# Two transformer layers with windowed attention on one core: projections of the second chunk on two PSUM banks, even score units in the first chunk, and a planner with four other durations and another table of priorities

## The chip, the core and the metric

The kernel runs on one core of a Trainium2 chip. The core has a matrix engine (TensorE, PE in the profile; its weight loads are listed apart as PEld), a vector engine (VectorE, DVE), a scalar engine (ScalarE, ACT), a general engine (GpSimd, POOL) and a queue engine (SyncE, SP) that issues nearly all DMAs here. Matmul results land in PSUM, eight banks of 512 fp32 columns on 128 partitions. The metric is the device time of one execution in microseconds (us). Three runs of the kernel before took 881.19, 881.58 and 882.57 us; the median is 881.58.

## The reference

The input x has 2048 rows of 576 numbers in bf16. Two layers with the same weights follow each other, each made of a mixer and an MLP:

```python
def _A_ref(x, wqkv, wo):                     # H = 32 heads of Dh = 18, window W = 256
    qkv = (x @ wqkv).reshape(B, S, 3, H, Dh).transpose(2, 0, 3, 1, 4)
    q, k, v = qkv[0], qkv[1], qkv[2]
    scores = einsum("bhqd,bhkd->bhqk", q, k) * Dh ** -0.5
    scores = where((i - j >= 0) & (i - j < W), scores, -1e9)
    o = einsum("bhqk,bhkd->bhqd", softmax(scores), v)
    return o.transpose(0, 2, 1, 3).reshape(B, S, D) @ wo
def _B_ref(x, w1, b1, w2, b2):               # F = 4608
    return gelu(layernorm(x) @ w1 + b1) @ w2 + b2
x = x + _A_ref(layernorm(x)); x = x + _B_ref(layernorm(x))     # twice
```

`_B_ref` normalizes once more inside, so that the MLP's input is normalized twice; the kernel does both in one step.

## The kernel before

**Tiles and chunks.** The rows are 16 tiles of 128. Four tiles make a chunk, and the two layers together make eight chunks, numbered k = 0 to 7; chunks 0 and 4 are the first of their layers. The residual stream stays on the chip in fp32 (`x_res`), and the weights of the MLP are streamed in from memory again for each chunk (`w1_load`, `w2_load`).

**Stages of a chunk.** `ln1` or `ln1_in` normalizes the four tiles (statistics on DVE at L678 and L682, the reciprocal root on POOL at L691 and L693, the normalized copy on DVE at L703, a second copy of its last 64 columns at L711, and a transposing DMA by SP at L727). `qkv` makes the projections of a tile: for each of q, k and v two outputs of 288 columns, each in a bank of its own. Chunks 0 and 1 use `two_out` (five matmuls of 128 rows for each output, L763); later chunks use two row halves of the array at once (L803). DVE takes each output out of its bank (L824 for q and k, L811 for v), and SP transposes q and k by DMA (L843). `E0` (chunk 0) and `E` (all others) do the attention for eight groups g of four heads: `scores` is one unit of work, up to 512 query columns for each of four heads (PE at L870), two exponentials on ACT (L879), each over two heads, and the masking of the blocks on the diagonal and at the window's far edge on POOL (L900). `pv` multiplies the weights by v (PE at L917), and DVE transposes and divides (L928, L931, L934, L938). `tail` multiplies by `wo` (L763), adds the residual (L980) and normalizes again for the MLP. `G_part` is a third of the first MLP matmul (L1033) with its gelu on ACT (L1043), `mm2` a third of the second (L1071) with its residual add on DVE (L980, at the very end L983).

**Banks.** Each unit of scores takes two pairs of banks out of three, (0,1), (2,3) and (4,5). The outputs of `pv` take one of 7, 6, 5, 4 in that order of preference, and so do projections, `tail` and `mm2`. For chunk 1 alone the projections may take nothing but bank 6, so that each output waits until DVE has emptied the one ahead of it. `G_part` may take any of the eight.

**The planner.** Nothing in the order is written out by hand. Each operation is added as a task with an engine, what it reads and writes, an assumed duration (`cost`, us), a latency and a priority. `Plan.schedule` then plays the kernel through with these durations: at each step it takes the task that can start first, and among those that start at the same time the one with the lowest priority number. PE tasks are of four kinds, `f` (whole array), `h` (two row halves), `r` (four row strips, the scores) and `c` (four column strips, `pv`); a change of kind is assumed to cost 0.095 us, and from 40 us on a table `PL.turn` adds a handicap to tasks that would change it. `PL.nudge` adds a number to the priority of each stage. Its keys are stage names: `ea2.1` is group 1 in the first part of the attention of chunk 2 (`ea`, `eb` and `ec` hold groups 0 to 2, 3 to 5, 6 and 7), `ea2.p1` its `pv`; `q2.1` the projections of tile 1 of chunk 2; `t2.1` the tail of that tile; `ga`, `gb`, `gc` and `ma`, `mb`, `mc` the three parts of the two MLP matmuls; `ln2` a normalization; a `+` marks the weight loads. What comes out is a fixed order for each engine; on the chip each engine runs through its own order and waits on semaphores. Where PE would be idle for long in the first 140 us, the planner puts in matmuls on zeros (L665).

**Units of the first chunk.** `units_of` cuts the scores of one group. In a middle chunk there are three units of 512 columns. In the first chunk of a layer the parts that would look back at rows before the start are dropped, and units of 384, 512 and 256 columns are left.

Of the kernel before, what the change touches and what calls it, by code (L numbers as in the profile page):

```python
# [417 lines left out]
def build_kernel(nc, A_x, A_wqkv, A_wo, B_x, B_w1, B_b1, B_w2, B_b2, out):  # L418
# [37 lines left out]
    PL = Plan(S, 8)  # L456
# [4 lines left out]
    PL.nudge = {"": -255.24, "b": -219.8, "ea0.0": 23.65, "ea0.1": -0.79, "ea0.2": 6.45, "ea0.p0": -38.42, "ea0.p1": 20.22,  # L461
# [88 lines left out]
    oq = sb("oq", [P, 16, 32], FP32)  # L550
# [3 lines left out]
    xn = sb("xn", [P, NXN, KD * 128], BF16)  # L554
# [710 lines left out]
```

## Time and profile before

One execution was profiled. It took 880.89 us, 0.69 us less than the median of the three runs; the profile's span is 879.2 us, and 1.69 us lie around it.

| Quantity | Value |
|---|---|
| Profiled execution | 880.89 us, span 879.2 us |
| PE busy | 861.2 us (98%), 9675 matmuls |
| ACT busy | 596.3 us (68%) |
| DVE busy | 414.2 us (47%) |
| POOL busy | 367.8 us (42%) |
| PE busy in the first 100 us | 91.03 us |
| PE busy from 100 to 865 us | 758.83 of 765 us |
| Granted TensorE clock | 1.00 throughout |

A busy share is the time in which an instruction of that engine was under way; matmuls overlap, so a PE that is always busy may still lose time at changes of kind. "Idle before" gives how long the engine stood still ahead of an instruction and which other engine's instruction ended that. An instruction's duration in the profile is longer than the step from one to the next where two of the same engine overlap.

### The profile page before, as it was taken

How to read it: one execution, taken by the hardware profiler on the slowest of the kernel's cores; microseconds unless marked ns; L12 is line 12 of the kernel's file. 1: busy time of each engine (PE TensorE's matmuls, PEld its weight loads, DVE VectorE, ACT ScalarE, POOL GpSimd, SP SyncE). 2: the span in 40 equal slices, each digit the busy share in tenths (PEclk: the TensorE clock that was granted, in tenths of full speed). 3: DMA queues.
4: the chain of work that ended last, by engine and by line, in shares of the span. 5: the costliest groups of instructions: out<-in, count | busy, mean ns of one | idle time of the engine just before them, and what ended most of it. 6: DMA issues, size and time to landing. Idle time of an engine off the chain costs nothing.

```text
span 879.2 us, 23104 instructions
## 1 busy us (share of the span) xinstructions
PE 861.2 (98%) x9675; PEld 507.4 (58%) x9675; DVE 414.2 (47%) x994; ACT 596.3 (68%) x741; POOL 367.8 (42%) x500
## 2 busy tenths in 40 slices
PE   9898999999999999999999999999999999999998
PEld 7444555556566565566655555655556555556665
DVE  6889423664237632476433943374233533262111
ACT  5976788858757696565774868729768589753443
POOL 3766554465234562254420845416444176231100
PEclk9999999999999999999999999999999999999999
DMA  7698435361585524936356262584425953445341
GB/s 193 141 196 187 113 114 135 110 165 52 163 164 126 136 63 157 181 108 179 103 131 186 62 180 84 150 174 111 155 82 136 226 123 104 136 130 171 104 159 50
DMA packets 181847, 119.53 MB, mean 136 GB/s; under 512 B 107440, under 2 KB 181744, under 8 KB 181744
## 3 DMA queue, kind: packets, MB, share of 16 engines
q1 hardware_dynamic: 181744, 118.05, 52.0%
q8 instruction: 77, 1.26, 0.6%
q14 instruction: 26, 0.21, 0.1%
HBM read 90.10 MB, written 2.36 MB: 105 GB/s over the span
## 4 chain that ended last, share of the span: by engine, by line
PE 80%; DVE 7%; DMA 4%; ACT 4%; issue 3%; POOL 2%; SPq 0%; DVEq 0%; POOLq 0%
PE ps L1033 31%; PE ps L1071 28%; PE ps L803 9%; PE ps L870 5%; PE ps L917 4%; PE ps L763 4%; ACT pT L879 3%; DVE xn L703 2%; DMA xnTm<-xn 2%; POOL pT L900 1%; DVE st_all L678 1%; DVE xn L711 1%; DMA xnTa<-xn 1%; DVE x_res L980 1%; ACT hT L1043 1%
## 5 line engine op out<-in xcount | busy, mean ns | idle before, releaser
L900 POOL TENSOR_SCALAR_AFFINE_SELECT pT<-pT 128x512 bf16<-128x512 bf16 (+1 forms) x368 | 287.8, 805 | 271.6 <-ACT pT L879 267.9
L879 ACT ACTIVATE pT<-ps 128x1024 bf16<-128x1024 f32 (+2 forms) x384 | 347.1, 972 | 51.5 <-PE ps L870 51.1
L1071 PE MATMUL ps<-w_sb,hT 128*128 128x288 bf16 x2208 | 298.5, 287 | 3.8 <-DVE x_res L980 2.0
L1043 ACT ACTIVATE hT<-ps,b1col 128x512 bf16<-128x512 f32 x276 | 168.4, 688 | 195.3 <-PE ps L1033 194.6
L1033 PE MATMUL ps<-xnTm,w_sb 64*128 64x512 bf16 x2592 | 292.8, 376 | 0.2 <-ACT pT L879 0.2
L1071 PEld LDWEIGHTS ps<-w_sb,hT 128*128 128x128 bf16 x2208 | 203.2, 98 | 84.6 <-issue 23.7
L1033 PEld LDWEIGHTS ps<-xnTm,w_sb 64*128 64x128 bf16 x2592 | 126.9, 94 | 141.9 <-issue 6.7
L980 DVE TENSOR_TENSOR x_res<-ps,x_res 128x288 f32<-128x288 f32 x224 | 99.1, 446 | 170.1 <-PE ps L1071 136.3
L928 DVE STREAM_TRANSPOSE oq<-ps 128x512 f32<-128x512 f32 x64 | 45.6, 712 | 112.1 <-PE ps L917 111.5
L803 PE MATMUL ps<-wqkv,xnTa 64*128 64x288 bf16 x1296 | 95.4, 283 | 2.5 <-DMA xnTa<-xn 0.9
L824 DVE CAST qn<-ps 128x288 bf16<-128x288 f32 x120 | 49.7, 449 | 80.6 <-PE ps L803 72.5
L803 PEld LDWEIGHTS ps<-wqkv,xnTa 64*128 64x128 bf16 x1296 | 61.1, 94 | 35.0 <-issue 6.4
L870 PE MATMUL ps<-qT,kT 32*128 32x384 bf16 (+2 forms) x1216 | 64.1, 276 | 2.0 <-ACT pT L879 1.7
L691 POOL TENSOR_SCALAR vtmp<-mv_all 128x1 f32<-128x1 f32 (+1 forms) x43 | 8.8, 206 | 130.6 <-DVE mv_all L682 129.1
L1049 POOL TENSOR_TENSOR x_res<-x_res,b2bc 128x576 f32<-128x576 f32 x32 | 40.7, 1293 | 43.8 <-ACT hT L1043 43.8
L678 DVE BATCH_NORM_STATS2 st_all<-x_res 128x6 f32<-128x288 f32 (+1 forms) x128 | 53.7, 443 | 1.7 <-DMA x_res<-in_A_x_dram 1.2
L917 PE MATMUL ps<-pT,vA 128*20 128x384 bf16 (+2 forms) x1408 | 50.4, 276 | 1.0 <-DVE qn L824 0.8
L703 DVE TENSOR_SCALAR xn<-x_res,mv_all,rstd 128x576 bf16<-128x576 f32 (+1 forms) x64 | 43.8, 685 | 13.8 <-DMA xnTm<-xn 5.7
L811 DVE CAST vA<-ps 128x288 bf16<-128x288 f32 x64 | 26.5, 448 | 40.5 <-PE ps L803 38.5
L763 PE MATMUL ps<-wo_sb,attT 128*128 128x288 bf16 x320 | 44.2, 287 | 0.6 <-DVE x_res L980 0.6
L870 PEld LDWEIGHTS ps<-qT,kT 32*128 32x128 bf16 x1216 | 19.4, 92 | 43.1 <-issue 30.3
L917 PEld LDWEIGHTS ps<-pT,vA 128*20 128x20 bf16 x1408 | 25.8, 90 | 23.1 <-issue 11.6
(47 smaller groups left out, 389.7 us busy)
## 6 DMA issues: line engine op xcount, KB each, us to landing
w_sb<-in_B_w_dram SPq DMA_DIRECT2D x48, 864.0 KB, 5.9
w_sb<-in_B_w_dram SPq DMA_DIRECT2D x48, 768.0 KB, 4.7
w_sb<-in_B_w_dram SPq DMA_DIRECT2D x96, 48.0 KB, 4.4
out_dram<-xn SPq DMA_DIRECT2D x16, 144.0 KB, 1.8
wqkv<-in_A_wqkv_dram SPq DMA_DIRECT2D x3, 576.0 KB, 5.3
x_res<-in_A_x_dram SPq DMA_DIRECT2D x3, 576.0 KB, 4.3
wo_sb<-in_A_wo_dram SPq DMA_DIRECT2D x4, 144.0 KB, 3.3
xnTm<-xn SPq DMA_TRANSPOSE x32, 2.6
```

The lines of the kernel that those rows point to most:

```text
L678: add("dve", lambda e, i=i, s=s: e.bn_stats(st_all[:, t, i, :], s[:, t, i * HB:(i + 1) * HB]), reads=res, writes=[f"st{t}_{i}"], cost=0.37 ...
L703: add("dve", lambda e: e.tensor_scalar(xn[:, sl, 0:D], s[:, t, :], mv_all[:, t, 0:1], rstd[:, t:t + 1], op0=ALU.subtract, op1=ALU.mult), r ...
L763: ins = e.matmul(bank(bs[o])[:, 0:HB], lhs(c), rhs(c, o * HB), start=(c == 0), stop=(c == KD - 1))
L803: ins = e.matmul(bank(bs[o])[:, 0:HB], xnTa[r:r + 64, c, i * 128:(i + 1) * 128], wqkv[r:r + 64, c, col:col + HB], start=(c == 4), stop=(ph ...
L870: ins = e.matmul(two(bs[j // 2])[:, j % 2, col:col + nq * 128], k_of(T0 + so)[0][32 * j:32 * j + 32, g, :], qs[32 * j:32 * j + 32, g, qo * ...
L879: add("act", lambda e, h2=h2: e.activation(pT[:, sl, 2 * h2:2 * h2 + 2, lo:hi], two(bs[h2])[:, :, lo:hi], ACT.Exp, scale=SCALE), reads=[bs ...
L900: add("pool", lambda e, ap=ap, pat=pat, sgn=sgn, kind=kind: e.affine_select(ap, ap, pattern=pat, compare_op=(ALU.is_ge if kind == "d" else ...
L917: ins = e.matmul(bank(bo)[32 * j:32 * j + VW, qo * 128:(qo + nq) * 128], vA[:, (T0 + so) % VS, 8 * j + g, :], pT[:, sl, j, col:col + nq * ...
L980: add("dve", lambda e: e.tensor_tensor(x_res[:, t, sl], bank(b)[:, 0:HB], x_old[:, t, sl], ALU.add), reads=[b] + ([f"xin{t}"] if first els ...
L1033: ins = e.matmul(bank(bks[i])[:, 0:n], w1_sb[r:r + 64, sls[i], col:col + 128], xnTm[r:r + 64, k % 2, c, 0:n], start=(c == 4), stop=(ph == ...
L1043: add("act", lambda e, ff=ff, hd=hd, bk=bk: e.activation(hd[:, 0:n], bank(bk)[:, 0:n], ACT.Gelu_apprx_tanh, bias=b1col[:, ff:ff + 1]), rea ...
L1071: ins = e.matmul(bank(b)[:, 0:HB], h_of(k, hf, fl)[0][:, i * 128:(i + 1) * 128], w2_sb[:, fl, hh * HB:(hh + 1) * HB], start=(fl == 0), sto ...
```

## The change

Four things change in the text of the kernel.

1. The projections of chunk 1 may take bank 6 or bank 7, not bank 6 alone.
2. In the first chunk of each layer (t0 = 0, chunks 0 and 4) the units of a group are 384, 384 and 384 columns: the 128 columns of the part (3, 3) move from the second unit to the third.
3. Assumed durations in the planner: the normalized copy at L703 from 0.67 to 0.53 us (from fp32) and from 0.45 to 0.43 us (from the bf16 input), its second copy at L711 from 0.38 to 0.24 us, the division of the attention's output at L934 from 0.60 to 0.45 us, the gelu at L1043 from 0.145 to 0.125 us plus 0.00087 us a column (at 512 columns from 0.590 to 0.570 us). The instructions themselves are the same.
4. The whole table `PL.nudge` is another one: 465 entries in place of 476, of which 48 have the value they had, nearly all of them for the last two chunks.

```diff
-    PL.nudge = {"": -255.24, "b": -219.8, "ea0.0": 23.65, "ea0.1": -0.79, "ea0.2": 6.45, "ea0.p0": -38.42, "ea0.p1": 20.22,
...
+    PL.nudge = {"": -3.97, "b": 31.08, "ea0.0": 10.46, "ea0.1": 43.28, "ea0.2": -4.02, "ea0.p0": 39.43, "ea0.p1": -87.35,
...
-            reads=res + [f"mv{t}", f"rstd{t}"], writes=[f"xn{sl}"], cost=0.67 if src is None else 0.45, lat=0.14, prio=prio)
+            reads=res + [f"mv{t}", f"rstd{t}"], writes=[f"xn{sl}"], cost=0.53 if src is None else 0.43, lat=0.14, prio=prio)
...
-                reads=res + [f"mv{t}", f"rstd{t}"], writes=[f"xd{sl}"], cost=0.38, lat=0.14, prio=prio)
+                reads=res + [f"mv{t}", f"rstd{t}"], writes=[f"xd{sl}"], cost=0.24, lat=0.14, prio=prio)
...
-                             wr, prio + 0.01 * n, after=dest, fill=(6,) if k == 1 else FILL)
+                             wr, prio + 0.01 * n, after=dest, fill=(6, 7) if k == 1 else FILL)
...
             us = [[(0, 0, 2, 0), (1, 1, 1, 256)], [(-1, 0, 2, 0), (-2, 0, 1, 256)]]
+        if t0 == 0:
+            us = [[(0, 0, 3, 0)], [(1, 1, 3, 128)], [(2, 2, 2, 256), (3, 3, 1, 128)]]
         us = [[p for p in u if t0 + p[0] >= 0] for u in us]
...
-            reads=["oq", f"ri{r}"], writes=[f"aq{g}"], cost=0.6, lat=0.14, prio=prio - 3)
+            reads=["oq", f"ri{r}"], writes=[f"aq{g}"], cost=0.45, lat=0.14, prio=prio - 3)
...
-                    reads=[bk, "b1"], writes=..., cost=0.145 + n * 0.00087, lat=0.17,
+                    reads=[bk, "b1"], writes=..., cost=0.125 + n * 0.00087, lat=0.17,
```

More of the change, by code (lines that the diff above doesn't have):

```diff
@@ L1044, in G_part @@
                                                                       bias=b1col[:, ff:ff + 1]),
-                    reads=[bk, "b1"], writes=[hn] + ([f"p{fl // 4}{x}" for x in ("h0", "h1", "m0", "m1", "m2")] if hn[1] == "p" else []), cost=0.145 + n * 0.00087, lat=0.17,
+                    reads=[bk, "b1"], writes=[hn] + ([f"p{fl // 4}{x}" for x in ("h0", "h1", "m0", "m1", "m2")] if hn[1] == "p" else []), cost=0.125 + n * 0.00087, lat=0.17,
                     fifo="act", prio=prio)
```

140 rows, old and new, of the table add are left out of this document.

## The prediction

> **What bounds the kernel now.** I read the page first (shares, the chain that ended last), then busy time by stage, then what PE waits for, then single stretches of the timeline.
>
> ```profile
> span 879.2 us, 23104 instructions
> ...
> PE 861.2 (98%) x9675; PEld 507.4 (58%) x9675; DVE 414.2 (47%) x994; ACT 596.3 (68%) x741; POOL 367.8 (42%) x500
> ...
> PE 80%; DVE 7%; DMA 4%; ACT 4%; issue 3%; POOL 2%; SPq 0%; DVEq 0%; POOLq 0%
> ```
>
> PE is on 80% of the chain. Busy time by stage (columns: stretch, its length, then busy of PE, PEld, DVE, ACT, POOL) shows that the rest sits at the start:
>
> ```profile
> 33.00:51.00 18.00, 14.39 (x189) 7.16 (x186) 17.39 (x42) 16.42 (x23) 14.01 (x21) 1.00 0.91 176
> 51.00:72.00 21.00, 20.82 (x269) 11.36 (x267) 16.79 (x41) 13.21 (x18) 11.51 (x15) 1.00 1.03 217
> 72.00:92.00 20.00, 17.57 (x247) 8.93 (x247) 19.08 (x51) 14.12 (x16) 14.50 (x23) 1.00 0.80 162
> ...
> 100.00:865.00 765.00, 758.83 (x8533) 445.19 (x8530) 333.60 (x786) 523.41 (x643) 306.99 (x404) 1.00 0.50 133
> ```
>
> DVE is full from 33 to 51 us, PE from 51 to 72, DVE again from 72 to 92, and from 100 to 865 PE stands still for 6.2 us in all. In that long part only two things can move: those 6.2 us, and what PE loses where the kind of matmul changes. The second is read off the chain, blocks of the same matmul in different lengths:
>
> ```profile
> 106.66 0.33 PE ps L870 x8
> 106.99 1.58 PE ps L1071 x12
> ...
> 119.22 0.84 PE ps L1071 x6
> ...
> 134.92 2.31 PE ps L1071 x18
> ```
>
> From 6 to 18 matmuls it is 1.47 us, 0.1225 us each; 6 of them would be 0.735, so 0.105 us belongs to the change of kind. Taking the trace's matmuls in order I count 526 changes, some 55 us. What PE waits for, from 100 to 865 us (total, times, longest):
>
> ```profile
> PE ps L1071 <- DVE x_res L980: 2.0, 3, 0.9
> PE ps L1071 <- DVE oq L928: 1.1, 1, 1.1
> PE ps L803 <- DMA xnTa<-xn: 0.9, 1, 0.9
> PE ps L1071 <- ACT hT L1043: 0.8, 1, 0.8
> ```
>
> **Part 1, a second bank for chunk 1's projections.** No instruction is added. What bank 6 alone costs, from 0 to 100 us:
>
> ```profile
> PE ps L763 <- DVE qn L824: 1.4, 4, 0.7
> ...
> PE ps L763 <- DVE vA L811: 1.0, 2, 0.7
> ```
>
> The most that can go is these 2.4 us. They lie between 34 and 51 us, where DVE has only 0.6 us free, and a bank doesn't take work off DVE: the nearest row for the other end is that full DVE, 0. A bank of lead is worth about one output, which the chain has at 0.72 us (five matmuls at L763), moved from the stretch 51 to 72, where PE is full, into the idle 3.6 us of PE before it. Between 0 and -2.4 I take -0.8, near that one output. What is late next is the DVE queue itself. Second: from 52 to 70 us the chain has ten single outputs of 0.72 us between other kinds. Two that run back to back save a change on either side, 2 x 0.105; five such pairs would be -1.05, none 0. I take -0.6. SP's q and k transposes of chunk 1 follow the casts and move with them, the same number. What this adds: bank 7 is the first choice of `pv`, which may now find it taken; see the rivals.
>
> **Part 2, even units.** Counted for one group of chunk 0. Scores: 384 + 512 + 256 columns against 3 x 384, the same 1152, and four matmuls for a part in both. Exponentials: the timeline has a pair of 1024 elements at 1.94 us (54.32), of 512 at 1.08 (57.30), of 768 at 1.51 (58.88), so 1.51 + 1.94 + 1.08 = 4.53 against 3 x 1.51 = 4.53. Masks: five instructions, one of them double, in both. Nothing is saved. Moved: the double mask (1.10 us against 0.64) is now in the last unit, so each group's `pv` may start 0.46 us later; seven times the next group's work covers it, and once, ahead of chunk 0's tail, it can show: +0.46. On the other side an exponential pair of 1.08 us is shorter than PE's way to the next unit, and ACT waited 1.04 us ahead of one of these; ACT's waits for scores from 33 to 51 us are 2.3 us in four. DVE, not ACT, is full there, so -0.5 is the end I give it. Value 0. In chunk 4 PE is full and all of this is off the path; if that cover is gone it is the same +0.46.
>
> **Part 3, four durations.** No instruction changes; the planner judges them otherwise. Four gelus in a row take 2.42 us at 688 ns each (124.40), so the step is (2.42 - 0.688) / 3 = 0.577 us: 0.570 is nearer than 0.590. The DVE ones (ns, least/median/largest):
>
> ```profile
> L703 DVE TENSOR_SCALAR xn<-x_res,mv_all,rstd x64: 378/579/1340, 5.2 to 792.7; 128x576 bf16<-128x576 f32 x48, 128x576 bf16<-128x576 bf16 x16
> L711 DVE TENSOR_SCALAR xn<-x_res,mv_all,rstd x60: 208/310/1268, 23.2 to 793.2; 128x64 bf16<-128x64 f32 x48, 128x64 bf16<-128x64 bf16 x12
> ...
> L934 DVE TENSOR_TENSOR attq<-oq,rinv x64: 436/457/1357, 34.9 to 778.3; 128x288 bf16<-128x288 f32 x64
> ```
>
> With some 0.07 us of overlap taken off, the medians give 0.51, 0.24 and 0.39. But by form the means are 716 (fp32), 488 (fp32) and 496 ns, hence 0.65, 0.42 and 0.43. So 0.45 at L934 is right where 0.60 was 0.17 too long, while at L703 with L711 the old sum 1.05 met the mean of 1.07, and the new 0.77 is 0.30 short for each tile. The long ones stand where POOL masks or computes rstd at the same time, at the change of chunks, and there they reach PE:
>
> ```profile
> 495.13 1.08 DVE L703 TENSOR_SCALAR xn<-x_res,mv_all,rstd 128x576 bf16<-128x576 f32 x1
> ...
> 496.13 0.62 DVE L711 TENSOR_SCALAR xn<-x_res,mv_all,rstd 128x64 bf16<-128x64 f32 x1
> ...
> 496.67 0.45 DVE L980 TENSOR_TENSOR x_res<-ps,x_res 128x288 f32<-128x288 f32 x1
> ...
> 497.17 1.64 PE L1071 MATMUL ps<-w_sb,hT 128*128 128x288 bf16 x12 [0.92 <-DVE x_res L980]
> ```
>
> PE waits 0.92 us for a bank whose emptying stands behind the slow copies in DVE's order. The add at L980, which reads PSUM, is never over 459 ns, and neither are the casts. The Trainium skill, "SBUF — State Buffer", section "Who interferes with whom", has VectorE and GpSimd share one pair of ports as an exclusive lock: a tensor_scalar in a two-port mode, or an instruction with two SBUF inputs against a GpSimd one that reads, stands still until the other has finished, and others never do. By that rule, which this trace bears out (1340 and 1357 ns at L703 and L934 against 459 at L980), a plan with the undisturbed durations is wrong just where POOL is busy, and it speaks against this part: by it alone the sum would be that of rival A.
>
> **Part 4, the order.** With another table each engine's order is another one; the trace can't show it, so it is bounded. Changes of kind: in the 16 stretches of 40 us between 120 and 760 us I count 17 to 32, scattered by about 4; over 16 that is 4 x 4 = 16 changes, 1.6 us either way, value 0. PE's waits: all 6.2 us could go; or the 0.30 us by which the plan is short reaches PE for four tiles at each of seven changes of chunk, 4 x 7 x 0.30 = +8.4. The three larger DVE and ACT rows above, 2.0 + 1.1 + 0.8 = 3.9, are waits for work queued behind instructions that the plan had timed wrong, L934 and the gelu among them; half of them gone is -2.0. Against it half a tile's shortfall at seven places, 7 x 0.15 = +1.0, nearer the low end because one tile in the shown stretch, over by 0.65 (1.08 + 0.62 against 1.05), is what made a wait of 0.92. Net -1.0. SP and POOL: some 120 transposes and 192 weight loads on SP's queue and the masks and rstd on POOL come in another order too; now they cost PE 0.9 us in one wait, and I leave that.
>
> **Sum**: -0.8 - 0.6 + 0 - 1.0 = -2.4 us. Against the profiled execution 880.89 - 2.4 = 878.5; that execution is 0.69 below the median of the runs, 881.58, so against the median 879.2, 0.27% faster.
>
> **Rivals.**
> *A. The short durations bring stalls (slower).* The plan expects the normalized tiles too early, and PE stands at each change of chunk behind DVE. For it: the 0.92 us above, with 1.07 us as the true mean. Against: the plan was as far off for single tiles before, and PE still lost only 6.2 us. Two of four tiles at seven places, 14 x 0.30 = 4.2, with the gain of part 1 kept: 881.6 + 4.2 - 1.4 = 884.4; all four, 888.6. It decides once more than 1.4 / 7 = 0.2 us is lost at each change.
> *B. Bank 7 is missed (slower).* A `pv` of chunk 0 that finds 7 and 6 taken goes to 5 or 4, the third pair of the scores, and the exponentials wait. The longest such wait from 33 to 51 us is 1.1 us; four of them +4.4, less 0.6: 885.4. From two on it eats part 1. Against: ACT has gaps and DVE, not ACT, is full.
> *C. Transposes land behind weight loads (slower).* A transposed tile lands after 2.7 us by the median and 7.5 at most; one such on the path is +4.8, less 1.4: 885.0. For it: two waits of 3.23 and 4.57 us for xnTm on the chain at 176 us. Against: PE is filled meanwhile.
> *D. Nothing lands.* DVE is full to 51 us and from 72 to 92, so the start ends when it did; the order is as good as the old one: 881.6, give or take 1.
>
> **How the numbers follow.** The forecast's case 0.46, A 0.26, B 0.07, C 0.07, D 0.14. The forecast's own range, 874 to 879.8, comes from both ends of part 1 in full (-3.45), half of the 6.2 (-3.1) and 1 us of changes of kind: 881.58 - 7.55 = 874.0. The whole range goes down a little further, to 873.5 (all 1.6 us of the changes: 873.4), and up to 887.5, three quarters of A in full (6.3) with the 1.6, less 1.4: 888.1, cut a little. What is left out is some 0.07 on either side. The three runs spread by 0.16%, so about 0.2%, 1.8 us, can be told from no change: faster 0.46, same 0.14, slower 0.26 + 0.07 + 0.07 = 0.40.
>
> **What the profile would show.** Part 1: PE's waits for L824 and L811 under 1 us, more blocks of ten at L763, PE busier from 33 to 51 us, and the first MLP matmul (now 89.80 us) about 1.4 us earlier. Part 2: 48 pairs of exponentials of 768 elements in chunks 0 and 4, none of 512. Parts 3 and 4: PE's waits from 100 to 865 us at some 5 us and 510 to 542 changes of kind. I am wrong if those waits grow beyond 8 us with L980, L928 or xnTm as releaser, if the start is no shorter, or if the changes of kind leave that band.

## The result, and the profile after

The changed kernel takes 887.06 us (median of five runs, 885.56 to 889.20); the kernel before, beside it, 881.80 us (881.19 to 882.57). The ratio is 1.0062 with a 95% interval of 1.0044 to 1.0081: slower by 5.3 us, where I had forecast 2.4 us faster. The time lies inside the range, just below its upper end of 887.5. The profiled execution of the changed kernel took 886.54 us, span 884.8. Part of the 5.3 us goes with the TensorE clock that was granted: the two runs of the changed kernel at a granted clock of 1.000 took 885.56 and 886.54 us, two at 0.998 887.06 and 888.58, one at 0.996 889.20, while all but one of the runs of the kernel before beside the experiments are at 1.000. Both profiled executions are at 1.00 throughout, so the 5.6 us between their spans owe nothing to it.

In the changed kernel's text the lines of the normalization and of the projections stand two lines higher: L701 is the normalized copy (L703 before), L709 its second copy (L711), L761 is `two_out` (L763), L801 and L809 the later projections and their cast to v (L803, L811). From L870 on the numbers are the same. In the experiments the lines are moved again: where an order is written out they stand 85 to 87 lines further down (L1158 for L1071), with only a part of the masks cut down two lines (L930 for L928); the tile names tell them apart.

The page of the changed kernel, its span, its busy times and the shares of the chain that ended last:

```profile
span 884.8 us, 23083 instructions
...
PE 858.3 (97%) x9669; PEld 511.9 (58%) x9669; DVE 418.6 (47%) x994; ACT 595.3 (67%) x741; POOL 367.3 (42%) x500
...
PE 78%; DVE 8%; ACT 5%; DMA 3%; issue 3%; POOL 2%; SPq 0%; DVEq 0%; POOLq 0%
```

Span less PE's busy time is the time in which PE stands still: 884.8 - 858.3 = 26.5 us, before 879.2 - 861.2 = 18.0. So PE stands still 8.5 us longer and is busy 2.9 us less, and 8.5 - 2.9 is the 5.6 us between the spans. Busy time by stage of the changed kernel (stretch, length, then busy of PE, PEld, DVE, ACT, POOL):

```profile
33.00:51.00 18.00, 16.29 (x202) 9.01 (x200) 16.64 (x45) 15.26 (x22) 14.23 (x19) 1.00 0.94 190
51.00:72.00 21.00, 18.54 (x280) 10.31 (x276) 16.86 (x40) 15.96 (x21) 13.00 (x18) 1.00 1.06 221
72.00:92.00 20.00, 17.47 (x250) 9.85 (x248) 19.80 (x52) 14.98 (x16) 15.88 (x24) 1.00 0.71 161
100.00:865.00 765.00, 751.83 (x8476) 445.87 (x8474) 337.74 (x784) 519.68 (x638) 306.91 (x404) 1.00 0.50 134
```

From 100 to 865 us PE now stands still for 765 - 751.83 = 13.2 us, 6.2 before: 7.0 of the 8.5 us are here. In the first 100 us it is busy for 89.45 us (91.03 before), 1.6 us less, yet that stretch loses nothing: the trace has fewer changes of kind there (77 against 92, and 15 x 0.105 = 1.6 us), and an equal amount of matmul work is behind PE at 99.54 us, before at 99.51.

What PE waits for from 100 to 865 us in the changed kernel (total, times, longest):

```profile
PE ps L870 <- DVE oq L928: 3.6, 2, 2.3
PE ps L1071 <- DVE x_res L980: 3.0, 3, 1.8
PE ps L1033 <- DVE oq L928: 1.3, 1, 1.3
PE ps L801 <- DVE x_res L980: 0.9, 1, 0.9
PE ps L1071 <- ACT hT L1043: 0.8, 1, 0.8
PE ps L870 <- DVE x_res L980: 0.8, 1, 0.8
```

All but one are waits for a bank that DVE has yet to empty; the one for ACT, 0.8 us at 800, the kernel before has too. By the starts of the matmuls PE's idle time lies at four changes of chunk: near 185 us (2.3 us in all, 1.9 before), 281 to 292 (2.7, 0.5 before), 393 to 406 (3.4, 0.9 before) and 495 to 505 (2.8, 0.9 before). The timeline of the changed kernel at the first of them (start, duration, engine, line, operation; in brackets what PE waited for):

```profile
179.64 2.31 POOL L900 TENSOR_SCALAR_AFFINE_SELECT pT<-pT 128x512 bf16<-128x512 bf16 x3
...
180.85 1.26 DVE L701 TENSOR_SCALAR xn<-x_res,mv_all,rstd 128x576 bf16<-128x576 bf16 x1
...
182.03 0.29 DVE L709 TENSOR_SCALAR xn<-x_res,mv_all,rstd 128x64 bf16<-128x64 bf16 x1
...
182.89 1.75 POOL L900 TENSOR_SCALAR_AFFINE_SELECT pT<-pT 128x1024 bf16<-128x1024 bf16 x2 [0.94 <-ACT pT L879]
182.97 1.19 DVE L701 TENSOR_SCALAR xn<-x_res,mv_all,rstd 128x576 bf16<-128x576 bf16 x1
184.07 0.60 DVE L709 TENSOR_SCALAR xn<-x_res,mv_all,rstd 128x64 bf16<-128x64 bf16 x1
184.59 0.70 DVE L928 STREAM_TRANSPOSE oq<-ps 128x512 f32<-128x512 f32 x1
...
185.44 0.40 PE L870 MATMUL ps<-qT,kT 32*128 32x256 bf16 x8 [2.27 <-DVE oq L928]
```

Two copies that start while POOL masks take 1.26 and 1.19 us (they read the bf16 input and were planned with 0.43); the transpose that empties PE's bank stands behind them, and PE stands still for 2.27 us. This is rival A of the prediction. The theory to test: the masks on POOL stretch the copies on DVE, DVE has no time left at the changes of chunk, and the new order, made with the short durations, has no slack for it.

### The profile page after: what moved, and what is told of

Its sections match the earlier page's. It is cut to its first block, busy times and chain, and to the rows that moved or that the text cites. A ratio compares the mean times of both kernels' runs of the same rounds, so it can differ in the third digit from the quotient of the medians.

```text
span 884.8 us, 23083 instructions
## 1 busy us (share of the span) xinstructions
PE 858.3 (97%) x9669; PEld 511.9 (58%) x9669; DVE 418.6 (47%) x994; ACT 595.3 (67%) x741; POOL 367.3 (42%) x500
## 4 chain that ended last, share of the span: by engine, by line
PE 78%; DVE 8%; ACT 5%; DMA 3%; issue 3%; POOL 2%; SPq 0%; DVEq 0%; POOLq 0%
PE ps L1033 31%; PE ps L1071 26%; PE ps L801 8%; PE ps L870 5%; PE ps L761 4%; ACT pT L879 4%; PE ps L917 4%; DVE xn L701 3%; DVE xn L709 2%; DMA xnTm<-xn 2%; POOL pT L900 1%; DVE x_res L980 1%; DVE st_all L676 1%; ACT hT L1043 1%; DMA xnTa<-xn 1%
## 5 line engine op out<-in xcount | busy, mean ns | idle before, releaser
L900 POOL TENSOR_SCALAR_AFFINE_SELECT pT<-pT 128x512 bf16<-128x512 bf16 (+1 forms) x368 | 287.6, 803 | 277.9 <-ACT pT L879 270.5
L879 ACT ACTIVATE pT<-ps 128x1024 bf16<-128x1024 f32 (+1 forms) x384 | 346.5, 973 | 59.5 <-PE ps L870 58.7
L1071 PE MATMUL ps<-w_sb,hT 128*128 128x288 bf16 x2208 | 296.8, 287 | 4.5 <-DVE x_res L980 3.0
L1043 ACT ACTIVATE hT<-ps,b1col 128x512 bf16<-128x512 f32 x276 | 168.2, 688 | 191.4 <-PE ps L1033 190.9
L1071 PEld LDWEIGHTS ps<-w_sb,hT 128*128 128x128 bf16 x2208 | 203.9, 98 | 83.5 <-issue 25.5
L1033 PEld LDWEIGHTS ps<-xnTm,w_sb 64*128 64x128 bf16 x2592 | 128.8, 94 | 140.8 <-issue 8.3
L980 DVE TENSOR_TENSOR x_res<-ps,x_res 128x288 f32<-128x288 f32 x224 | 99.0, 446 | 172.2 <-PE ps L1071 139.3
L928 DVE STREAM_TRANSPOSE oq<-ps 128x512 f32<-128x512 f32 x64 | 45.6, 713 | 124.7 <-PE ps L917 124.5
L801 PE MATMUL ps<-wqkv,xnTa 64*128 64x288 bf16 x1296 | 93.8, 283 | 5.1 <-DVE rinv L931 1.9
L801 PEld LDWEIGHTS ps<-wqkv,xnTa 64*128 64x128 bf16 x1296 | 62.5, 94 | 35.6 <-issue 7.0
L870 PE MATMUL ps<-qT,kT 32*128 32x384 bf16 (+2 forms) x1216 | 64.1, 276 | 6.9 <-DVE oq L928 3.6
L701 DVE TENSOR_SCALAR xn<-x_res,mv_all,rstd 128x576 bf16<-128x576 f32 (+1 forms) x64 | 45.0, 705 | 11.8 <-DMA xnTm<-xn 3.9
L870 PEld LDWEIGHTS ps<-qT,kT 32*128 32x128 bf16 x1216 | 19.6, 92 | 48.2 <-issue 32.5
L761 PE MATMUL ps<-wo_sb,attT 128*128 128x288 bf16 x320 | 43.0, 287 | 0.0
L809 DVE CAST vA<-ps 128x288 bf16<-128x288 f32 x64 | 26.5, 449 | 34.2 <-PE ps L801 30.9
```

Source lines behind the costliest of these rows:

```text
L701: add("dve", lambda e: e.tensor_scalar(xn[:, sl, 0:D], s[:, t, :], mv_all[:, t, 0:1], rstd[:, t:t + 1], op0=ALU.subtract, op1=ALU.mult), r ...
L761: ins = e.matmul(bank(bs[o])[:, 0:HB], lhs(c), rhs(c, o * HB), start=(c == 0), stop=(c == KD - 1))
L801: ins = e.matmul(bank(bs[o])[:, 0:HB], xnTa[r:r + 64, c, i * 128:(i + 1) * 128], wqkv[r:r + 64, c, col:col + HB], start=(c == 4), stop=(ph ...
L870: ins = e.matmul(two(bs[j // 2])[:, j % 2, col:col + nq * 128], k_of(T0 + so)[0][32 * j:32 * j + 32, g, :], qs[32 * j:32 * j + 32, g, qo * ...
L879: add("act", lambda e, h2=h2: e.activation(pT[:, sl, 2 * h2:2 * h2 + 2, lo:hi], two(bs[h2])[:, :, lo:hi], ACT.Exp, scale=SCALE), reads=[bs ...
L900: add("pool", lambda e, ap=ap, pat=pat, sgn=sgn, kind=kind: e.affine_select(ap, ap, pattern=pat, compare_op=(ALU.is_ge if kind == "d" else ...
```

## The experiments

In most of them the planner's run is replaced by its result, written out: the order of every engine and the bank of every output are those of the kernel before or of the changed kernel, operation by operation, and the edit alone is new. Where masks are cut down or the second copy is shortened, the planner runs with every assumed duration as it was and gives the same order. Where a new plan was made instead, it is said.

**Masks cut down, in both orders.** Each mask at L900 is done on 8 columns of one head only, so most of the masking is left out and the attention is another one.

```diff
-                ap, ap, pattern=pat, compare_op=...
+                ap[:, 0:1, 0:8], ap[:, 0:1, 0:8], pattern=[[0, 1], [sgn, 8]], compare_op=...
```

In the changed kernel:

> The changed kernel with its order kept, but each mask on POOL shrunk to 8 columns of one head (so the attention isn't masked: work left out). POOL then hardly runs beside DVE's normalized copies. Theory 1 (the copies, slowed by POOL beyond the planned 0.53 and 0.24 us, keep PE waiting at the changes of chunk): the mean of the fp32 copy at L701 falls from some 720 to under 600 ns, PE's idle time from 100 to 865 us falls from 13.2 to 4 us or less, and the time from 887.1 to about 877 us. Theory 2 (the order is bad in itself, whatever the copies take): the idle time stays at 10 us or more and the time at 884 us or more.

In the kernel before:

> The kernel before with its order kept and the same shrunken masks (attention not masked). Theory 1: PE's idle time from 100 to 865 us falls from 6.2 to about 3 us, the time from 881.8 to 878 or 879 us, and the changed order without masks is then 1 to 4 us faster than this one, since it has 27 changes of matmul kind fewer. Theory 2: this one gains about as much as the changed kernel does, and stays 4 to 6 us ahead of it.

Measured beside the same 882.17 us of the kernel before: 873.01 us in the new order (870.61 to 876.09; ratio 0.9896, 0.9871 to 0.9922) and 876.76 in the old one (874.56 to 878.29; 0.9935, 0.9917 to 0.9953). Groups of DVE by line and form (count, busy us, mean ns) of the changed kernel:

```profile
L980 DVE TENSOR_TENSOR x_res<-ps,x_res 128x288 f32<-128x288 f32 x224 | 99.0, 446 | 172.2 <-PE ps L1071 139.3 <-PE ps L761 32.0
L701 DVE TENSOR_SCALAR xn<-x_res,mv_all,rstd 128x576 bf16<-128x576 f32 x48 | 35.6, 743 | 6.6 <-DMA xnTm<-xn 3.9 <-POOL rstd L691 2.2 <-DVE st_all L676 0.3
...
L709 DVE TENSOR_SCALAR xn<-x_res,mv_all,rstd 128x64 bf16<-128x64 f32 x48 | 23.5, 491 | 0.0
```

and of the same with the masks cut down:

```profile
L980 DVE TENSOR_TENSOR x_res<-ps,x_res 128x288 f32<-128x288 f32 x224 | 99.8, 449 | 173.7 <-PE ps L1071 140.1 <-PE ps L761 32.1
...
L701 DVE TENSOR_SCALAR xn<-x_res,mv_all,rstd 128x576 bf16<-128x576 f32 x48 | 27.3, 570 | 8.3 <-DMA xnTm<-xn 6.4 <-POOL rstd L691 1.0 <-DMA xnTa<-xn 0.3
L709 DVE TENSOR_SCALAR xn<-x_res,mv_all,rstd 128x64 bf16<-128x64 f32 x48 | 14.6, 306 | 0.0
```

The copies fall from 743 to 570 and from 491 to 306 ns, while the add at L980, which reads PSUM, stays at 446 to 449. PE's idle time from 100 to 865 us falls to 3.0 us, in the old order from 6.2 to 2.3. This is theory 1, and in both orders somewhat more than I had expected. The masks also stand ahead of the reciprocal roots in POOL's queue, but the time for which DVE stands idle for those ahead of the copies in these rows is only 2.2 us in all, 1.0 with the masks cut down. So the masks cost the new order 887.06 - 873.01 = 14.0 us and the old one 882.17 - 876.76 = 5.4. Without them the new order is 3.75 us the faster: the order was good, but for copies that last 0.57 and 0.31 us.

**Which masks.** In the changed kernel, once only the masks of groups 0 to 2 of chunks 1 to 7 are cut down (the stages `ea`, those at a change of chunk: 123 of 368 instructions), once all the others.

```diff
+            if PL.stage.startswith("ea") and k:
+                ap, pat = ap[:, 0:1, 0:8], [[0, 1], [sgn, 8]]
```

> The changed kernel, order kept, with the masks shrunk to 8 columns of one head only in the first three groups of chunks 1 to 7 (their attention isn't masked: work left out). These 63 units of scores are the ones whose masks run at the changes of chunk, beside the normalized copies; the other masks stay. If the loss is POOL holding up those copies: most of what all masks gave (14.0 us) comes back with these alone, 875 to 879 us, and PE's idle time from 100 to 860 us falls below 5 us. If POOL's masks cost time anywhere (their latency ahead of pv, their load as such): about their share of the masks, a third, 882 us or more.

With all the others cut down (the same with `not`):

> The counterpart: the masks of all other groups shrunk (all of chunk 0, groups 3 to 7 of the others; their attention isn't masked), those of the first three groups of chunks 1 to 7 kept. If the loss lies at the changes of chunk: little comes back, 884 to 887 us, and the idle time stays above 11 us. If it is the masks' load anywhere: two thirds of the 14 us, 879 us or less.

Measured: 873.20 us (870.49 to 877.64; ratio 0.9904, 0.9874 to 0.9934) with those at the changes of chunk cut down, 889.05 us (884.22 to 889.66; 1.0071, 1.0043 to 1.0099) with all the others. Busy time from 100 to 860 us, first with those at the changes cut down:

```profile
100.00:860.00 760.00, 758.00 (x8539) 449.91 (x8536) 320.21 (x785) 524.89 (x645) 245.01 (x404) 1.00 0.50 134
```

then with all the others cut down:

```profile
100.00:860.00 760.00, 746.79 (x8416) 443.18 (x8411) 335.99 (x782) 518.65 (x636) 186.70 (x405) 1.00 0.49 132
```

PE's idle time is 2.0 us in the first and 13.2 us in the second, as in the changed kernel (746.83 busy). A third of the masks gives back the whole 14 us, the other two thirds, 120 us of POOL's time in this stretch, nothing that shows: three of those four runs had a granted clock of 0.996, and the one at 1.000 took 884.22 us, 1.3 to 2.3 us less than the changed kernel's two at 1.000. The stretch shown above, in the timeline of the kernel with the first third cut down:

```profile
178.62 0.42 DVE L701 TENSOR_SCALAR xn<-x_res,mv_all,rstd 128x576 bf16<-128x576 bf16 x1
178.96 0.29 DVE L709 TENSOR_SCALAR xn<-x_res,mv_all,rstd 128x64 bf16<-128x64 bf16 x1
...
180.28 0.43 DVE L701 TENSOR_SCALAR xn<-x_res,mv_all,rstd 128x576 bf16<-128x576 bf16 x1
180.62 0.30 DVE L709 TENSOR_SCALAR xn<-x_res,mv_all,rstd 128x64 bf16<-128x64 bf16 x1
...
180.83 0.71 DVE L930 STREAM_TRANSPOSE oq<-ps 128x512 f32<-128x512 f32 x1
...
182.28 0.40 PE L870 MATMUL ps<-qT,kT 32*128 32x256 bf16 x8
```

The same two tiles' copies take 0.42, 0.29, 0.43 and 0.30 us; from the start of the first to the transpose it is 2.2 us (178.62 to 180.83) where it was 3.7 (180.85 to 184.59), and the matmul waits for nobody.

**Is it the place in DVE's queue?** In the changed kernel DVE's order alone is another: the instructions that empty banks are moved ahead of the copies, at the changes of chunk and elsewhere (some 440 of DVE's 994 instructions stand at another place, by up to 13 places). In a second kernel POOL's order is changed with it.

> The changed kernel with another order on DVE alone: every instruction, every bank and the order of PE, ACT, POOL and SP stay; on DVE single instructions are moved by a few places, above all the ones that empty banks (L980, L928) ahead of normalized copies (L701, L709) that POOL may hold up. Theory 1 (PE waits for banks whose emptying is queued behind slowed copies): PE's waits for L980, L928 and L931 from 100 to 865 us fall from some 9 to under 4 us though the copies stay slow (a mean of 650 ns or more at L701), and the time falls from 887.1 to between 874 and 881 us. If the copies' length itself is what counts (the normalized tiles come too late, whatever is queued), the time stays at 885 us or more.

> The same with POOL's order changed too (masks, rstd and the b2 adds moved by a few places), PE, ACT and SP as in the changed kernel. Theory 1: as the last one or 1 to 3 us better, 872 to 880 us, with shorter copies at L701 if masks no longer stand beside them. If the copies' length is what counts, 885 us or more.

Measured: 887.44 us (886.09 to 889.43; 1.0067, 1.0047 to 1.0087) and 885.54 us (884.09 to 886.07; 1.0036, 1.0023 to 1.0049). The second is 1.5 us faster, which its interval hardly tells from the changed kernel's; the first gained nothing. What PE waits for from 100 to 860 us in the first:

```profile
PE ps L888 <- DMA xnTa<-xn: 2.4, 2, 1.7
PE ps L1158 <- DVE x_res L1067: 1.8, 2, 1.4
PE ps L1120 <- DMA xnTm<-xn: 1.8, 2, 1.5
PE ps L1158 <- DVE oq L1015: 1.3, 1, 1.3
```

The waits for DVE's transposes and adds became shorter, and waits for the normalized tiles themselves (`xnTa`, `xnTm`) took their place: what goes ahead of the copies makes the copies late. So DVE seems to be short of time there, whichever instruction comes last. In the changed kernel it is busy for 11.89 of the 12 us from 176 to 188 and 13.99 of the 14 from 492 to 506.

**A shorter second copy.** L709 copies 2 columns in place of 64, so that part of the normalized input is left out; in both orders.

```diff
-            add("dve", lambda e: e.tensor_scalar(xn[:, sl, D:KD * 128], s[:, t, 512:D], ...
+            add("dve", lambda e: e.tensor_scalar(xn[:, sl, D:D + 2], s[:, t, 512:514], ...
```

> The changed kernel with the second copy at L709 cut to 2 of its 64 columns (the transposed tile then holds stale values there: work left out), order and masks kept. It takes time off DVE at the changes of chunk, some 0.1 to 0.2 us for each of 60 copies and what POOL's lock adds to it, and moves nothing. Theory 3 (DVE is full at each change of chunk, so what counts is the time of the copies, not their place in the queue): 4 tiles at seven places times 0.1 to 0.2 us is 3 to 6 us, of which most is seen: 882 to 885 us, idle time of PE from 100 to 860 us from 13.2 down to 8 to 10 us. If only waits behind POOL count, not the copy's own time: within 1 us of 887.1.

> The kernel before with the same cut. Theory 3: the same time comes off DVE, but this order was planned with 0.77 to 1.05 us a tile more or less as the chip has it, and PE stands idle for only 6.2 us there: 1 to 3 us faster than 881.8, less than the changed kernel gains. If only waits behind POOL count: within 1 us.

Measured: 888.34 us in the new order (886.56 to 891.43; 1.0060, 1.0041 to 1.0079), 881.71 in the old one (880.97 to 882.94; 0.9997, 0.9987 to 1.0006). A miss, and the group of L709 in the new order shows why:

```profile
L709 DVE TENSOR_SCALAR xn<-x_res,mv_all,rstd 128x2 bf16<-128x2 f32 x48 | 22.9, 479 | 0.0
```

A copy of 2 columns takes 479 ns on average where one of 64 took 491. Its length is not its columns, so this edit took no time off DVE (336.7 us busy from 100 to 865, 337.7 without the edit).

**The second copy on ACT.** So it has to leave DVE altogether. ACT makes it, from the normalized tile, at the same place in its own order; the masks stay as they are.

```diff
-            add("dve", lambda e: e.tensor_scalar(xn[:, sl, D:KD * 128], s[:, t, 512:D], mv_all[:, t, 0:1], rstd[:, t:t + 1],
-                                                  op0=ALU.subtract, op1=ALU.mult),
-                reads=res + [f"mv{t}", f"rstd{t}"], writes=[f"xd{sl}"], ...
+            add("act", lambda e: e.copy(xn[:, sl, D:KD * 128], xn[:, sl, 512:D]), reads=[f"xn{sl}"], writes=[f"xd{sl}"], ...
```

> The changed kernel, every engine's order and every bank kept, with the second copy of the last 64 columns (the group of L709) taken off DVE: ACT makes it, from the normalized tile itself, at the same place in its own order. If DVE, full beside the masks at the changes of chunk, is what the new order lacks, it gets back up to two of these copies of 0.49 us at each of seven changes, at most 4 x 0.49 x 7 = 13.7 us in all, and PE's idle time from 100 us on, 13.2 us, falls to some 6: 880 us, and 876 at best. The rival: only the place in the order counts, and ACT, which now waits for each tile, holds up the exponentials behind it: 887 or more.

> The same edit in the kernel before, its order kept. DVE was full at its changes of chunk too, but PE stood still for 6.2 us only: between 879 us (half of that gone) and 884 (ACT's waits for the tiles reach PE).

The first of these had 386 outputs in other banks than the changed kernel, against what its expectation says, so two more kernels separate the two:

> In a_actdup 386 outputs of matmuls had also been given another PSUM bank than in the changed kernel, unlike what its expectation says. Here the second copies go to ACT alone, with every engine's order and every bank those of the changed kernel. If the relief of DVE is what gave 3.5 us there, the time is 882.5 to 885 and PE's idle time from 100 to 860 us some 6 us, as there; if it was the banks, it is 887 with 13 us idle.

> The changed kernel with the banks of a_actdup and nothing else: the second copies stay on DVE. If the banks count for nothing, 886 to 888 and 13 us idle from 100 to 860 us; if they gave the 3.5 us, 883.5.

Measured: 883.52 us with both (879.60 to 885.73; 1.0017, 1.0002 to 1.0033), 883.34 with the copies on ACT alone (880.45 to 886.24; 1.0017, 1.0003 to 1.0031), 888.79 with the banks alone (885.10 to 889.63; 1.0071, 1.0047 to 1.0096). So the relief of DVE gives back 3.7 us and the banks none. In the old order the same edit changes nothing: 881.75 (880.41 to 882.75; 0.9998, 0.9988 to 1.0007). Busy time from 100 to 860 us in the new order, copies on ACT and banks kept:

```profile
100.00:860.00 760.00, 753.51 (x8498) 445.39 (x8494) 317.54 (x736) 529.46 (x688) 309.03 (x407) 1.00 0.51 135
```

The longest waits of PE in the same stretch of the same kernel:

```profile
PE ps L956 <- ACT pT L965: 3.3, 4, 1.2
PE ps L1157 <- ACT hT L1129: 1.0, 1, 1.0
```

PE's idle time there is 6.5 us in place of 13.2, and no wait for DVE is left among the large ones. That 6.7 us became 3.7 is the price on the other side: in the first 100 us PE is now busy for 87.89 us, 89.45 without the edit, and waits 4.0 us for exponentials, 1.9 without it; they stand behind the copies on ACT, which itself waits up to 2.74 us for a tile. From the end of the longest of PE's waits (2.88 us, up to 89.7 us) the granted clock is at half for 3.41 us, and with both the work that was done at 99.5 us is done at 102.2. Leaving the copies of the first two chunks on DVE should avoid that, but it wasn't tried.

**Parts alone.** The even units in the kernel before, its order and banks kept:

> The kernel before with the even units alone (384, 384, 384 columns in chunks 0 and 4): each engine's order and each bank as before, operation by operation. Part 2 as predicted: between -0.5 and +0.5 us, so 881.3 to 882.3 us. Rival: the double mask in the last unit holds up each group's pv, and each of eight groups loses up to 0.46 us: up to 885.5 us.

Measured: 884.16 us (883.29 to 885.40; ratio 1.0024, 1.0013 to 1.0034), 2.0 us slower than the kernel before beside it. The timeline has the double mask of the last unit holding up a `pv` by more than the 0.46 us I had priced:

```profile
38.00 0.67 PE L1004 MATMUL ps<-pT,vA 128*20 128x384 bf16 x16 [1.09 <-POOL pT L987]
```

That is one wait of 1.1 us. In the first 100 us PE's waits for exponentials (3.0 us, 2.3 before) and the projections' for the q and k casts (2.3 us, 1.4 before) grew as well; how the 2.0 us divide among these was not shown.

The old units in the changed kernel, its order and banks kept:

> The changed kernel with the old units (384, 512, 256 columns) in chunks 0 and 4; each engine's order and each bank stay those of the changed kernel. If even units are bad by themselves, as in the order before (+2.0 us), this is about 885 us. If the order was made for them, it is slower than 887.1 us by 2 to 8 us, lost in the first 100 us, where the second unit must now wait for the fourth tile's k and q.

Measured: 888.75 us (887.39 to 889.03; 1.0072, 1.0048 to 1.0097), which the intervals don't tell from the changed kernel's 1.0062. The units cost something in the order that was not made for them, and gain nothing that can be measured in the one that was.

Bank 7 for chunk 1's projections in the kernel before, the order kept; the edit of the change, with six outputs on bank 7 in place of 6:

> The kernel before with banks 6 and 7 for chunk 1's projections, each taking the one that is free earlier; each engine's order and all other banks as before. Part 1 as predicted: -0.8 us from the waits, none of the -0.6 from fewer changes, so about 881 us. Rival B (bank 7 is missed by pv, which keeps it here): PE waits at L917 and L870 in the first 100 us grow by several us, 884 us or more.

Measured: 885.25 us (884.78 to 886.17; 1.0039, 1.0025 to 1.0054), 3.1 us slower. The other way round, bank 6 alone in the changed kernel, its order kept, with 14 outputs on 6 in place of 7:

> The changed kernel with chunk 1's projections on bank 6 alone again; each engine's order and all other banks stay those of the changed kernel. If the second bank is bad by itself, as it was in the order before (+3.1 us), this is faster than 887.1 us by some 3 us. If the changed order was made for two banks, PE runs into the full bank in the first 100 us: its waits for the casts at L822 and L809 come back, 5 to 15 us more, 892 to 902 us.

Measured: 900.07 us (899.06 to 901.09; 1.0205, 1.0166 to 1.0244). What PE waits for in the first 100 us of it:

```profile
PE ps L848 <- DVE qn L909: 6.2, 13, 1.2
PE ps L848 <- DVE oq L1015: 2.8, 4, 0.9
```

The new order uses the second bank: without it the projections wait 6.2 us for the q and k casts, where in the kernel before they waited 1.4.

**The durations alone, planned anew.** The kernel before with the four new durations and its own table of priorities, and the changed kernel with the four old durations and the new table:

> The kernel before with the four new durations alone, planned anew with the old table of priorities. If the short durations are the whole cause, the order changes a little at the changes of chunk and the time is that of the changed kernel, 885 to 890 us. If a table of priorities fits only the durations it goes with, the order falls apart: 895 us or more, with PE's waits spread over the whole span.

> The changed kernel with the four old durations, planned anew with the new table, two banks and even units. If the short durations are the whole cause, this is at or below the time before, 882 us or less. If the table fits only its own durations: 895 us or more.

One execution of each took 916.35 and 907.49 us, at a granted clock of 0.988 and 0.992; by the stretches at half clock in their traces, 20.5 and 13.7 us, that is some 10 and 7 us, an estimate. Both lose more than any theory of the durations asked for even so; in both PE is busy for less than 740 of the 760 us from 100 to 860. Neither table fits the other durations here, so planning anew can't tell what the durations are worth by themselves; that they are what made the new order as tight as it is was therefore not shown apart from the table. What the order lacks, time on DVE beside the masks, was.

## Why the prediction was wrong

**Part 1 (-0.8 and -0.6).** The mechanism was there: the waits of 2.4 us for L824 and L811 that I had listed are gone from the projections of chunk 1, and 15 changes of kind fewer in the first 100 us are 1.6 us, more than the 0.6 I took. The start is still no shorter, 99.54 against 99.51 us for the same matmul work, and the first MLP matmul starts at 91.1 us, not ahead of 89.8: PE waits at other places in place of it, in rows that the kernel before hadn't: 1.9 us for L931, 1.2 for `xnTa`, 1.0 for L928. I had named this as one of three ways to be wrong, and the other two came as well (waits above 8 us, and changes of kind outside 510 to 542). The value at the other end, 0, was the right one; DVE, full from 72 to 92 us as before (19.80 of 20), is what I had priced that end by. Bank 7 by itself costs 3.1 us in the order that was not made for it. Rival B's way has a part in it: in that trace `pv` waits 1.7 us for the q and k casts in the first 100 us, 0.8 before, and it reads nothing of theirs, so what it waits for is a bank. The rest was not shown.

**Part 2 (0).** The sums on ACT hold: in the changed kernel there are 96 exponentials of 768 elements, 48 pairs, in chunks 0 and 4 and none of 512. But the ends, -0.5 and +0.46, were too close: alone in the old order the edit costs 2.0 us. I had taken seven of the eight groups as covered by the next group's work, and the wait of 1.09 us at 38 us lies in the middle of chunk 0.

**Part 3.** The reading was right (but for the casts, which reach 461 ns and not 459), and the value taken was not. I had 0.30 us of shortfall for each tile from fp32 input; in the changed kernel the two means are 743 + 491 = 1234 ns, with 0.07 of overlap off each 1.09 us, against 0.77 planned: 0.32. The sentence of the Trainium skill that I had weighed, "SBUF — State Buffer", section "Who interferes with whom", spoke against the change, and the runs agree with it: copies from and to SBUF lose 173 and 185 ns on average to the masks, the add that reads PSUM none (446 and 449 ns).

**Part 4 (-1.0), the step that failed.** It was the term "half a tile's shortfall at seven places, 7 x 0.15 = +1.0, nearer the low end", against -2.0 for the older waits. PE's idle time from 100 to 865 us rose by 7.0 us, not fell by 1.0. The count was short, too. I took four tiles at seven changes, 28; from 100 us on the trace has 44 pairs of copies from fp32, since at most changes the tiles are normalized for the MLP and for the next chunk's projections. At 0.30 us each the upper end is 13.2 us and not 8.4, and about half of that reached PE, at four changes. I chose the low end because in the kernel before one tile, 0.65 over, had made a wait of 0.92. That was evidence of the slack in the old order, and the change replaces that order: a plan that believes in shorter copies probably also puts other work closer behind them, which was not shown apart from the table. The half of the 3.9 us that was to go didn't: the waits for `x_res` at L1071 went from 2.0 to 3.0, those for `oq` from 1.1 in one place to 5.5 in four. I had put these waits down to durations that the plan had wrong (L934, the gelu). The old order with its masks cut down shows another cause: both rows are gone there (only the 0.8 for the gelu stays), so it was the masks that made them.

Also missed, on the other side: changes of kind. I took 0 with 1.6 us either way; they went from 518 to 491 (counted in the same way in both traces, the matmuls on zeros among them; the 526 of the prediction was 8 too many), and 27 x 0.105 = 2.8 us, close to the 2.9 us by which PE's busy time fell. With +8.5 of idle time, which is 7.0 from 100 to 865 us and 1.5 elsewhere, this makes the 5.6 us between the spans.

**The rivals.** A was what happened, and its place (DVE at the changes of chunk), its releasers (L980 and L928) and its size (884.4 to 888.6 us) were as written, the size by luck in part, since the count of tiles behind it was too low; I gave it 0.26. The threshold I wrote for it, 0.2 us lost at each change of chunk on average, was passed with 7.0 / 7 = 1.0. C can be set aside: no DMA is among the waits of the changed kernel above 0.5 us from 100 to 865 us. D was right for the start alone.

## What to carry to other kernels

A planner's durations should be those that an instruction has beside the work it will run beside, not those it has alone: here a copy of 0.57 us costs 0.74 on average and up to 1.4 us next to another engine's masks, and an order built on the short value gave 14 us away where it was the better one by 3.75 us undisturbed. Where the plan is to change, the waits of the old order say how much slack the old order had, not how large the disturbance is; price the disturbance itself, at all its places, unless something other than the old order absorbs it: here 13.2 us by that count, of which 7.0 reached PE. A suspected contention is tested quickly by cutting down the other engine's work with the order kept, and a suspected lack of time on an engine by moving one of its instructions elsewhere, since a change of place in its queue, or fewer columns, may leave its total as it was.

## What was not expected of the hardware

A DVE copy of 2 columns lasts nearly as long as one of 64: 479 and 491 ns on average, 288 and 309 by the median. And cutting down the 123 masks at the changes of chunk, 72 us of POOL's busy time in all (367.3 to 295.5), was worth 14 us, while cutting down the 245 others, 142 us of it (to 224.8), was worth next to nothing.

The granted clock was at half for stretches of 3.41 us, or twice that, in most of the traces. In the one with the changed kernel's order and other banks they start at 61.2 and 187.5 us, 1.3 and 0.8 us behind the ends of PE waits of 1.95 and 2.27 us; across the second, this trace's lag behind that of the changed kernel, which has the same waits and no such stretch, grows by 1.7 us and stays. So a wait may cost PE more than its own length; whether the waits bring these stretches on was not tested.
